# Attention chunks with float32 products with the values, two heads side by side, and 1/sum ahead of the transposition

## The chip, the core and the metric

The kernel runs on one core of a Trainium2 chip. The core has a matrix engine (TensorE, PE in the profile; its weight loads are listed as PEld), VectorE (DVE), ScalarE (ACT), GpSimd (POOL) and SyncE (SP), which here only issues transfers. TensorE writes to PSUM banks; the other three read and write the on-chip memory and, GpSimd excepted, PSUM. The metric is the device time of one execution in microseconds, as the median of repeated runs. Before the change it is 716.54 us (three runs, 716.34 to 716.68).

## What is computed

Attention with four sink keys and a window of 128 keys, in 4 batches and 8 heads of width 64 over 768 positions, followed by an expert layer with a squared ReLU. All data are float32.

```python
scores = scale * np.matmul(q, k.transpose(0, 1, 3, 2))
keep = is_sink | in_window
scores = np.where(keep, scores, -1000000000.0)
a = np.exp(scores - np.max(scores, axis=-1, keepdims=True))
a = a / (np.sum(a, axis=-1, keepdims=True) + 1e-09)
attn = np.matmul(a, v)            # (4, 8, 768, 64), then tokens x 512
h = x @ w_in                      # 3072 x 512 by 512 x 2048
r = np.maximum(h, 0.0)
g = s * (r * r) + b
out = g @ w_out
```

## The kernel before

**Tiling.** The 3072 tokens are worked in eight chunks of 384 (`CH`), half a batch each, in the order `ORDER`. A chunk of the first half of a batch is called half 0, one of the second half 1. Each chunk has an attention part, which leaves its result transposed in `k.x` (512 features x 384 tokens, as a high and a low part), and an expert part. The expert part of a chunk (`moe_steps`) consists of 16 blocks `l1(f)`, twelve products of 384 columns each (L610), and 16 blocks `l2(f)`, nine products of 512 columns each (L630), which alternate.

**Precision.** The fast products take float32r operands. A float32 number is therefore split into a rounded high part and the rest, and a product is made of high x high, high x low and low x high. Products of plain float32 operands also exist (L555 and L509 in the plain chunks); each is listed with two records in the profile.

**Order.** The instructions are recorded in program order on each engine, and a scheduler moves some of them. While the expert part of chunk c is recorded, the attention of chunk c+1 is recorded between its blocks in slots, some 33 for 30 blocks (the loop at L785). The first two chunks use the class `Plain`, which has float32 products throughout; chunks 2 to 7 use `attn_slots`. In a plain chunk, `values` multiplies the values two heads side by side: the head `hh` writes partitions 64*hh to 64*hh+63 of one bank (L555), and products of the same width spread 1/sum (L560).

**A slot in `attn_slots`.** The work on one head and 128 queries is a unit, 24 a chunk. In slot t, the kernel records what is due ahead (loads and `prep_head`), then `unit_c` for unit t-7 (`LC`), `unit_a` for unit t, `unit_b` for unit t-4 (`LB`), the ends of a group of heads, and the transposition `turn` for the next slot's `unit_b`.

- `unit_a` makes the scores (L308, L309), the masked minimum on VectorE (L313), the exponential with its row sum on ScalarE (L319), adds the two window squares into one on GpSimd (L322), since they don't overlap, and copies the eight sink columns to `psk` (L323).
- `turn` transposes the 128 x 128 square on TensorE (L329).
- `unit_b` splits the transposed square into its two triangles on VectorE (L342, into `two`), rounds the high part on ScalarE (L344) and makes the low part on GpSimd (L345), both into `hl`. After a pair's last unit it makes 1/sum (L354 to L358) and puts it into `psk`.
- `unit_c` multiplies by the values, in two visits a head: with the second unit (L382, four products in half 1, two in half 0) and with the third (L374 and two L382). The values stand side by side as high and low part in `vv` (128 wide), so that high and low come out in different partitions; L389, L390 and L392 add them.
- `sinks` adds the sink keys' part (L406, L407); `scaled` spreads 1/sum over the partitions by a product with `sel` (L413), multiplies (L414), and splits the result into `k.x` (L415, L416).

PSUM has eight banks: five rotate among the scores, `h`, `o`, `ts`, `os` and `zb` (pool `psA`, function `ps`), and three hold `po`. A bank is used again when its last reader is done.

Of the kernel before, what the change touches and what calls it, by code (L numbers as in the profile page):

```python
# [37 lines left out]
LB, LC, LD, LDL, L2 = 4, 7, ((3, 4), (6, 7)), ((2, 2), (3, 3)), 2  # L38
# [3 lines left out]
def tile_kernel(ctx, tc, qT, kT, k0, v, vsk, n_sink, window, w, s, b, out):  # L42
# [91 lines left out]
    def constants2():  # L134

        spread = wk.tile([P, 2, P], F32, tag="y", name="spread", bufs=3)
        nc.gpsimd.memset(spread, 0.0)
        for j in range(4):
            row = spread[96:P, j // 2].rearrange("p (a d) -> p a d", a=2)
            nc.gpsimd.affine_select(out=row, in_=row, pattern=[[1, 2], [0, D]], compare_op=ALU.not_equal, fill=1.0,  # L140
                                    base=2 * j, channel_multiplier=-1)
        nc.scalar.copy(sel, spread)
# [135 lines left out]
    def prep_head(k, h):  # L278
# [11 lines left out]
        hd.vv = wk.tile([P, 4, P], F32R, tag="vv", name="vv", bufs=VB)  # L290
        a, c = (0, D) if h % 2 == 0 else (D, 0)
        n = hd.nkb
        nc.scalar.copy(hd.vv[:, :n, a:a + D], hd.v[:, :n, :])
# [556 lines left out]
```

## Time and profile before

| | us |
|---|---|
| median of three runs | 716.54 |
| the profiled execution | 715.33 |
| its span | 713.6 |
| TensorE busy | 693.0 |
| VectorE busy | 500.6 |
| ScalarE busy | 469.4 |
| GpSimd busy | 385.3 |

The span runs from the first to the last instruction of the profiled execution; the rest of its time lies around it. The granted clock of TensorE was full (0.998) throughout. Up to about 130 us the first two chunks' attention and the preparation of the weights run; from there to about 635 us the expert part of chunks 1 to 6 runs with the attention of chunks 2 to 7 between its blocks; the last chunk's expert part stands alone. The time of a step on TensorE is read as the distance between the starts of two blocks in the timeline, since a matmul's listed duration overlaps that of the next. A line of a timeline stands for several records where it says x12.

### The profile page before, as it was taken

How to read it: one execution, taken by the hardware profiler on the slowest of the kernel's cores; microseconds unless marked ns; L12 is line 12 of the kernel's file. 1: busy time of each engine (PE TensorE's matmuls, PEld its weight loads, DVE VectorE, ACT ScalarE, POOL GpSimd, SP SyncE). 2: the span in 40 equal slices, each digit the busy share in tenths (PEclk: the TensorE clock that was granted, in tenths of full speed). 3: DMA queues.
4: the chain of work that ended last, by engine and by line, in shares of the span. 5: the costliest groups of instructions: out<-in, count | busy, mean ns of one | idle time of the engine just before them, and what ended most of it. 6: DMA issues, size and time to landing. Idle time of an engine off the chain costs nothing.

```text
span 713.6 us, 12060 instructions
## 1 busy us (share of the span) xinstructions
PE 693.0 (97%) x3908; PEld 613.8 (86%) x3908; DVE 500.6 (70%) x1186; ACT 469.4 (66%) x1153; POOL 385.3 (54%) x671
## 2 busy tenths in 40 slices
PE   8799999999999999999999999999999999999996
PEld 4477877899989998899999999899998999899895
DVE  6899979488865798657885788657786588743321
ACT  6999975578845786467764787556774677733222
POOL 2356635379843899336671788625773488700000
PEclk9999999999999999999999999999999999999999
DMA  7873140322112122021111121111221221000001
GB/s 283 355 269 130 34 155 27 108 66 57 57 56 75 42 81 55 17 82 58 50 57 65 51 72 51 35 64 53 57 63 37 80 66 42 1 30 15 1 1 49
DMA packets 27382, 52.63 MB, mean 74 GB/s; under 512 B 3504, under 2 KB 15536, under 8 KB 25392
## 3 DMA queue, kind: packets, MB, share of 16 engines
q1 hardware_dynamic: 27312, 51.79, 22.0%
q8 instruction: 33, 0.54, 0.3%
q14 instruction: 37, 0.30, 0.1%
HBM read 45.49 MB, written 6.29 MB: 73 GB/s over the span
## 4 chain that ended last, share of the span: by engine, by line
PE 76%; DVE 6%; ACT 3%; POOL 2%; issue 1%; DMA 1%; POOLq 0%; ACTq 0%; DVEq 0%
PE h L610 32%; PE po L630 32%; PE o L382 3%; PE sc L308 2%; PE sc L309 2%; PE sc L329 2%; DVE w L230 1%; DMA w<-in_w 1%; DVE w L220 1%; PE o L374 1%; DVE wt L219 1%; POOL hl L345 1%; POOL kl L289 1%; PE os L406 1%; PE ts L397 1%
## 5 line engine op out<-in xcount | busy, mean ns | idle before, releaser
L610 PE MATMUL h<-x,w 128*128 128x384 f32 x1536 | 297.6, 342 | 6.0 <-DVE w L230 2.6
L630 PE MATMUL po<-w,g 128*128 128x512 f32 x1152 | 295.9, 402 | 0.0
L610 PEld LDWEIGHTS h<-x,w 128*128 128x128 f32 x1536 | 264.8, 188 | 14.3 <-DVE w L230 3.3
L630 PEld LDWEIGHTS po<-w,g 128*128 128x128 f32 x1152 | 209.8, 189 | 43.7 <-issue 1.6
L616 DVE SCALAR_TENSOR_TENSOR r<-h,sb,r 128x384 f32<-128x384 f32 x112 | 68.9, 615 | 78.8 <-ACT r L613 77.9
L613 ACT ACTIVATE r<-h 128x384 f32<-128x384 f32 x128 | 62.9, 491 | 90.6 <-PE h L610 81.1
L619 DVE SCALAR_TENSOR_TENSOR g<-r,sb,g 128x384 fp32r<-128x384 f32 x112 | 91.5, 817 | 31.3 <-ACT g L618 29.7
L345 POOL TENSOR_TENSOR hl<-two,hl 128x256 fp32r<-128x256 f32 x128 | 102.3, 801 | 15.4 <-ACT hl L344 13.3
L322 POOL TENSOR_TENSOR sm<-sm 128x128 f32<-128x128 f32 x128 | 67.4, 527 | 61.2 <-ACT sm L319 59.0
L319 ACT ACTIVATE sm<-sm,negm 128x264 f32<-128x264 f32 (+1 forms) x144 | 72.1, 500 | 28.5 <-DVE negm L313 27.3
L618 ACT ACTIVATE g<-r,sb 128x384 fp32r<-128x384 f32 x112 | 69.1, 617 | 22.7 <-DVE r L616 21.9
L206 POOL TENSOR_TENSOR w<-w 128x256 int32<-128x256 int32 x60 | 48.6, 840 | 54.3 <-DVE zf L532 15.1
L289 POOL TENSOR_TENSOR kl<-kraw,kh 128x528 fp32r<-128x528 f32 (+1 forms) x48 | 60.8, 1266 | 20.7 <-ACT kh L287 20.4
L344 ACT CAST hl<-two 128x256 fp32r<-128x256 f32 x128 | 50.5, 394 | 26.0 <-DVE two L342 25.7
L342 DVE TENSOR_TENSOR two<-sc,split 128x256 f32<-128x256 f32 x128 | 53.1, 417 | 5.8 <-POOL hl L345 5.5
L323 POOL COPY psk<-sm 128x24 f32<-128x24 f32 x144 | 35.5, 247 | 17.1 <-ACT sm L319 17.0
L382 PE MATMUL o<-hl,vv 128*128 128x256 f32 (+1 forms) x256 | 44.3, 275 | 0.0
L382 PEld LDWEIGHTS o<-hl,vv 128*128 128x128 f32 x256 | 39.6, 188 | 3.2
L288 DVE TENSOR_TENSOR qs<-qraw,qs 64x384 fp32r<-64x384 f32 x48 | 39.7, 827 | 3.5 <-ACT qs L284 1.9
L313 DVE CUSTOM_DVE_ANT_0 sm<-sc,msk 128x264 f32<-128x264 f32 (+1 forms) x80 | 32.0, 400 | 14.0 <-PE sc L309 13.4
L308 PE MATMUL sc<-kh,qs 128*128 128x264 f32 (+1 forms) x144 | 41.6, 291 | 0.0
L313 DVE CUSTOM_DVE_ANT_0 sm<-sc,m_all 128x264 f32<-128x264 f32 x64 | 27.3, 426 | 20.1 <-PE sc L309 18.4
(139 smaller groups left out, 924.0 us busy)
## 6 DMA issues: line engine op xcount, KB each, us to landing
w<-in_w SPq DMA_DIRECT2D x15, 1024.0 KB, 10.5
kraw<-in_kT SPq DMA_DIRECT2D x32, 264.0 KB, 2.6
out<-ot SPq DMA_DIRECT2D x24, 256.0 KB, 2.0
qraw<-in_qT SPq DMA_DIRECT2D x24, 192.0 KB, 2.4
vraw<-in_v SPq DMA_DIRECT2D x16, 256.0 KB, 2.7
kraw<-in_kT SPq DMA_DIRECT2D x16, 200.0 KB, 2.4
vsraw<-in_vsk SPq DMA_DIRECT2D x24, 64.0 KB, 2.1
vraw<-in_v SPq DMA_DIRECT2D x8, 192.0 KB, 2.4
```

Of the source, the lines that this page charges most:

```text
L289: nc.gpsimd.tensor_tensor(out=hd.kl[:, :kw], in0=hd.k[:, :kw], in1=hd.kh[:, :kw].bitcast(F32), op=ALU.subtract)
L313: nc.vector.tensor_tensor_reduce(out=sm[:, :n], in0=sc[:, :n], in1=m, scale=-0.125, scalar=BIG, op0=ALU.add, op1=ALU.min, accum_out=negm[: ...
L319: nc.scalar.activation(sm[:, :n], sm[:, :n], AF.Exp, bias=negm[:, uu], scale=-1.0, accum_out=pp.zz[:, i, hh:hh + 1])
L322: nc.gpsimd.tensor_tensor(out=sm[:, c1:c1 + P], in0=sm[:, p1:p1 + P], in1=sm[:, c1:c1 + P], op=ALU.add)
L345: nc.gpsimd.tensor_tensor(out=lo, in0=both, in1=hi.bitcast(F32), op=ALU.subtract)
L382: nc.tensor.matmul(hd.o[:, q0:q0 + n * P], hd.vv[:, kb, :], hd.hl[:, t, c0 * P:(c0 + n) * P], start=(hd.n == 0), stop=(i == BLK - 1 and kb ...
L610: nc.tensor.matmul(h[:, :CH], weight[f][:, 0, wi, cc * P:(cc + 1) * P], x[xi][:, cc, :], start=(i == 0), stop=(i == 11))
L613: nc.scalar.activation(r, h[:, :CH], AF.Relu, scale=1.0 / WUP)
L616: nc.vector.scalar_tensor_tensor(out=hr, in0=h[:, :CH], scalar=sw_ap, in1=r, op0=ALU.mult, op1=ALU.mult)
L618: nc.scalar.activation(gg[:, 0, :], hr, AF.Identity, bias=b_ap, scale=1.0)
L619: nc.vector.scalar_tensor_tensor(out=gg[:, 1, :], in0=hr, scalar=b_ap, in1=gg[:, 0, :].bitcast(F32), op0=ALU.add, op1=ALU.subtract)
L630: nc.tensor.matmul(po[tb], gg[:, gi, tsl], weight[f][:, 1, wi, :], start=(f == 0 and i == 0), stop=(f == NF - 1 and i == 2))
```

## The change

It affects chunks 2 to 7.

- `unit_c` no longer works on rounded parts. It multiplies float32 squares by float32 values, once for both heads of a pair, when the second head's unit is due: each head writes its 64 partitions of one bank `o`, as in the plain chunks. The copies and additions of high and low parts (`vv`, `hl`, L389 to L392) go; `o` is copied once.
- A new step `norm`, in every second slot, makes 1/sum for two units on VectorE, multiplies their squares by it on ScalarE ahead of the transposition, and their sink columns on GpSimd, where these were copied before. `scaled`, `sel` and the places of 1/sum in `psk` go; `sinks` makes `k.x` itself.
- The values of a pair are loaded later, in a step of their own, six slots into the pair, with two buffers.
- `unit_b` and `unit_c` come one slot later (`LB` 5, `LC` 8), with five buffers `sm` instead of four. `hl` becomes `tt`, one for both heads.

```diff
-SMB, HLB = 4, 2
+SMB, HLB, VL = 5, 2, 6
-LB, LC, LD, LDL, L2 = 4, 7, ((3, 4), (6, 7)), ((2, 2), (3, 3)), 2
+LB, LC, LD, LDL, L2 = 5, 8, (3, 5), (2, 2), 2
...
+    def load_values(k, pr):
+
+        pp = k.pairs[pr]
+        pp.v = wk.tile([P, 4, 2, D], F32, name="v", tag="vv", bufs=2)
+        nc.sync.dma_start(pp.v[:, :pp.nkb], v[k.b, pr, :, pp.v0:pp.v0 + pp.nkb])
...
-        hd.vv = wk.tile([P, 4, P], F32R, tag="vv", name="vv", bufs=VB)
-        a, c = (0, D) if h % 2 == 0 else (D, 0)
-        n = hd.nkb
-        nc.scalar.copy(hd.vv[:, :n, a:a + D], hd.v[:, :n, :])
-        nc.gpsimd.tensor_tensor(out=hd.vv[:, :n, c:c + D], in0=hd.v[:, :n, :], in1=hd.vv[:, :n, a:a + D].bitcast(F32),
-                                op=ALU.subtract)
...
+    def norm(k, *two):
+
+        z = k.pairs[two[0][0] // 2].z
+        j0 = two[0][0] % 2 * BLK + two[0][1]
+        jj = slice(j0, j0 + 2)
+        nc.vector.tensor_scalar(out=z[:, 1, jj], in0=z[:, 0, jj], scalar1=1e-9, scalar2=None, op0=ALU.add)
+        nc.vector.reciprocal(out=z[:, 2, jj], in_=z[:, 1, jj])
+        for j, (h, i) in enumerate(two):
+            pp = k.pairs[h // 2]
+            sm, c0, _, s0 = k.cc[(h, i)]
+            rz = z[:, 2, j0 + j:j0 + j + 1]
+            nc.scalar.mul(sm[:, c0:c0 + P], sm[:, c0:c0 + P], rz)
+            nc.gpsimd.tensor_scalar(out=pp.psk[:, i, :12 * NS].rearrange("p (t x) -> p t x", t=3)[:, :, h % 4 * NS:(h % 4 + 1) * NS],
+                                    in0=sm[:, s0:s0 + NS].unsqueeze(1).to_broadcast([P, 3, NS]), scalar1=rz, scalar2=None, op0=ALU.mult)
...
         if p0 is not None:
-            both = wk.tile([P, 2 * P], F32, tag="two", name="two", bufs=2)
             nc.vector.tensor_tensor(out=both.rearrange("p (s c) -> p s c", s=2), in0=tp.unsqueeze(1).to_broadcast([P, 2, P]), in1=split,
                                     op=ALU.mult)
-            nc.scalar.copy(hi, both)
-            nc.gpsimd.tensor_tensor(out=lo, in0=both, in1=hi.bitcast(F32), op=ALU.subtract)
         else:
-            nc.scalar.copy(hi, tp)
-            nc.vector.tensor_tensor(out=lo, in0=tp, in1=hi.bitcast(F32), op=ALU.subtract)
...
+            nc.scalar.copy(both[:, P:], tp)
...
+        if h % 2 == 0 or i == 0:
+            return
         if i == 1:
...
+            pp.o = ps("o")
+        mm = [(cur - 1, 2 * i - 1, 2)]
         if i == 1 and k.half == 1:
             mm.append((0, 0, 1))
+        if i == BLK - 1:
+            mm.insert(0, (cur, 2 * i + 1, 1))
         for kb, c0, n in mm:
...
+            q0 = c0 // 2 * P
+            for hh in range(2):
+                nc.tensor.matmul(pp.o[hh * D:(hh + 1) * D, q0:q0 + n * P], pp.v[:, kb, hh], pp.t[:, hh, c0 * P:(c0 + n) * P],
+                                 start=(i == 1 and kb == cur - 1), stop=(i == BLK - 1 and kb == cur - 1))
...
-        zb = ps("zb")
-        nc.tensor.matmul(zb[:, :CH], sel[:, pr % 2], pp.xs, start=True, stop=True)
-        nc.vector.tensor_tensor(out=pp.x, in0=zb[:, :CH], in1=pp.x, op=ALU.mult)
...
+                if t % 2 == 0 and 0 < t <= n:
+                    norm(k, *units[t - 2:t])
```

The line numbers of the changed kernel differ: its score products are L298 and L299, `turn` is L331, the products with the values L363, `l1` L578 and `l2` L598. First TensorE in a half-1 chunk, where a head's values are multiplied before the change; `o` is the bank, `hl` the split squares, `vv` the values, `sc` the scores:

```order
L382 MATMUL o<-hl,vv 128x256 x2
L382 MATMUL o<-hl,vv 128x128 x2
L308 MATMUL sc<-kh,qs 128x264
L309 MATMUL sc<-kl,qs 128x264
L329 MATMUL sc<-identr,sm 128x128
L630 MATMUL po<-w_696,g 128x512 x9
L374 MATMUL o<-hl,vv 128x256
L382 MATMUL o<-hl,vv 128x256 x2
L308 MATMUL sc<-kh,qs 128x264
L309 MATMUL sc<-kl,qs 128x264
L329 MATMUL sc<-identr,sm 128x128
```

After it, where both heads of a pair are multiplied (`tt` holds their squares, `v` their values):

```order
L363 MATMUL o<-tt,v 64x256 x2
L363 MATMUL o<-tt,v 64x128 x2
L298 MATMUL sc<-kh,qs 128x264
L299 MATMUL sc<-kl,qs 128x264
L331 MATMUL sc<-identr,sm 128x128
L598 MATMUL po<-w_615,g 128x512 x9
L363 MATMUL o<-tt,v 64x128 x2
L363 MATMUL o<-tt,v 64x256 x2
L298 MATMUL sc<-kh,qs 128x264
L299 MATMUL sc<-kl,qs 128x264
L331 MATMUL sc<-identr,sm 128x128
```

The two visits of each head have become two visits a pair, each between full-width products of the expert part and of the scores; the products are 64 wide.

Now ScalarE in such a chunk before the change, with the exponential L319, the high parts L344, the Relu L613 and the bias copy L618 of `l1`:

```order
L319 ACTIVATE sm,zz<-sm,negm 128x264
L344 CAST hl<-two 128x256
L319 ACTIVATE sm,zz<-sm,negm 128x264
L344 CAST hl<-two 128x256
L613 ACTIVATE r<-h 128x384
L287 CAST kh<-kraw 128x528
L618 ACTIVATE g<-r,sb 128x384
L319 ACTIVATE sm,zz<-sm,negm 128x264
L344 CAST hl<-two 128x256
```

And after it, with the exponential L307, the Relu L581 and the bias copy L586 (`zz` holds the sums and 1/sum):

```order
L307 ACTIVATE sm,zz<-sm,negm 128x264
L324 ACTIVATE sm<-sm,zz 128x128 x2
L581 ACTIVATE r<-h 128x384
L280 CAST qs<-qraw 64x384
L307 ACTIVATE sm,zz<-sm,negm 128x264
L586 ACTIVATE g<-r,sb 128x384
L283 CAST kh<-kraw 128x528
L307 ACTIVATE sm,zz<-sm,negm 128x264
L324 ACTIVATE sm<-sm,zz 128x128 x2
L581 ACTIVATE r<-h 128x384
```

A high part per unit has gone; in every second slot two multiplications (L324) stand between an exponential and the Relu.

## Rows read from the trace of the kernel before

**Rows 1.** The page, busy us of each engine, share of the span and instructions.

```profile
PE 693.0 (97%) x3908; PEld 613.8 (86%) x3908; DVE 500.6 (70%) x1186; ACT 469.4 (66%) x1153; POOL 385.3 (54%) x671
```

**Rows 2.** Busy time by engine, stage with half-1 attention (stretch, us, busy us, records).

```profile
215.36:300.69 85.33, 84.84 (x479) 77.74 (x479) 62.73 (x148) 58.03 (x149) 58.27 (x104) 1.00 0.19 56
```

**Rows 3.** Chain that ended last, stage without attention (start us, us, what).

```profile
645.80 2.11 PE po L630 x9
647.91 2.12 PE h L610 x12
```

**Rows 4.** TensorE's timeline, half-1 attention, blocks alone (start us, us, engine line op).

```profile
234.13 2.36 PE L610 MATMUL h<-x,w 128*128 128x384 f32 x12
...
236.60 2.35 PE L630 MATMUL po<-w,g 128*128 128x512 f32 x9
...
239.52 2.37 PE L610 MATMUL h<-x,w 128*128 128x384 f32 x12
...
242.36 2.35 PE L630 MATMUL po<-w,g 128*128 128x512 f32 x9
```

**Rows 5.** TensorE's timeline, two visits of a half-0 chunk.

```profile
324.01 0.40 PE L382 MATMUL o<-hl,vv 128*128 128x256 f32 x2
324.25 0.28 PE L308 MATMUL sc<-kh,qs 128*128 128x264 f32 x1
...
326.71 0.28 PE L374 MATMUL o<-hl,vv 128*128 128x256 f32 x1
...
327.07 0.23 PE L308 MATMUL sc<-kh,qs 128*128 128x136 f32 x1
```

**Rows 6.** TensorE's timeline, a product with `sel`.

```profile
282.18 0.34 PE L413 MATMUL zb<-xsk,sel 128*128 128x384 f32 x1
282.35 0.27 PE L329 MATMUL sc<-identr,sm 128*128 128x128 f32 x1
```

**Rows 7.** TensorE's timeline, plain chunk, two visits of 64-wide products.

```profile
73.79 2.28 PE L630 MATMUL po<-w,g 128*128 128x512 f32 x9
76.00 1.52 PE L555 MATMUL o<-tf,vf 128*64 128x384 f32 x12
77.35 0.82 PE L560 MATMUL zb<-identr,zf 128*64 128x128 f32 x12
78.10 2.36 PE L610 MATMUL h<-x,w 128*128 128x384 f32 x12
80.30 0.49 PE L544 MATMUL tp<-identr,smf 128*128 128x128 f32 x3
...
108.66 2.25 PE L610 MATMUL h<-x,w 128*128 128x384 f32 x12
...
115.14 0.51 PE L610 MATMUL h<-x,w 128*128 128x384 f32 x2
```

**Rows 8.** Groups by line and shape, TensorE (busy us, mean ns | idle before).

```profile
L555 PE MATMUL o<-tf,vf 128*64 128x256 f32 x16 | 2.4, 379 | 0.0
...
L555 PE MATMUL o<-tf,vf 128*64 128x128 f32 x16 | 1.6, 273 | 0.0
```

**Rows 9.** Waits of TensorE, 131 to 640 us; then groups of weight loads.

```profile
PE h L610 <- DVE y L414: 1.9, 3, 1.1
...
L329 PEld LDWEIGHTS sc<-identr,sm 128*128 128x128 f32 x144 | 20.2, 140 | 1.7 <-DVE r L616 1.6
```

**Rows 10.** TensorE's timeline, plain chunk, one form of product twice.

```profile
80.83 0.92 PE L509 MATMUL sc<-kf,qf 64*128 64x384 f32 x4
...
99.10 1.31 PE L509 MATMUL sc<-kf,qf 64*128 64x384 f32 x4
```

**Rows 11.** Groups by line, page (VectorE, GpSimd); ScalarE by shape, 130 to 640 us.

```profile
L342 DVE TENSOR_TENSOR two<-sc,split 128x256 f32<-128x256 f32 x128 | 53.1, 417 | 5.8 <-POOL hl L345 5.5
...
L289 POOL TENSOR_TENSOR kl<-kraw,kh 128x528 fp32r<-128x528 f32 (+1 forms) x48 | 60.8, 1266 | 20.7 <-ACT kh L287 20.4
...
L275 ACT CAST vs<-vsraw 128x128 fp32r<-128x128 f32 x24 | 6.5, 293 | 0.0
```

More of the change, by code (lines that the diff above doesn't have):

```diff
@@ L30 @@
 LOADS = 8
-SMB, HLB = 4, 2
+SMB, HLB, VL = 5, 2, 6
 WARM0 = 14
 NARROW, NEARLY = 2, 8
-RB, VB = 1, 2
+RB = 1
 E0 = 16
@@ L134, in constants2 @@
     def constants2():
[L136 to L142, printed above, removed]
         nc.vector.tensor_tensor(out=tmp[:, :NS], in0=low[:, :NS], in1=snk[:, :NS], op=ALU.mult)
@@ L331, in unit_b @@
     def unit_b(k, h, i, tp):
-        sm, c0, p0, _ = k.cc.pop((h, i))
-        hd = k.heads[h]
-        if i == 0:
-            hd.hl = wk.tile([P, 2, 2 * CH], F32R, name="hl", tag="hl", bufs=HLB)
-        a, z = (P if p0 is None else 0), 2 * P
-        hi, lo = (hd.hl[:, t, i * z + a:(i + 1) * z] for t in range(2))
+        _, _, p0, _ = k.cc.pop((h, i))
+        pp = k.pairs[h // 2]
+        if h % 2 == 0 and i == 0:
+            pp.t = wk.tile([P, 2, 2 * CH], F32, name="tt", tag="hl", bufs=HLB)
@@ L360, in unit_c @@
     def unit_c(k, h, i):
-        hd = k.heads[h]
         pp = k.pairs[h // 2]
         cur = i if k.half == 0 else i + 1
+        if h % 2 == 0 or i == 0:
+            return
         if i == 1:
-            hd.o = ps("o")
-            hd.n = 0
-        mm = []
-        if i == BLK - 1:
-            c0 = (2 * i + 1) * P
-            nc.tensor.matmul(hd.o[:, i * P:], hd.vv[:, cur, :], hd.hl[:, :, c0:c0 + P], start=False, stop=False)
-        if i > 0:
-            mm.append((cur - 1, 2 * i - 1, 2))
+            pp.o = ps("o")
@@ L377, in unit_c @@
+        mm = [(cur - 1, 2 * i - 1, 2)]
         if i == 1 and k.half == 1:
             mm.append((0, 0, 1))
+        if i == BLK - 1:
+            mm.insert(0, (cur, 2 * i + 1, 1))
         for kb, c0, n in mm:
-            for t in range(2):
-                q0 = c0 // 2 * P
-                nc.tensor.matmul(hd.o[:, q0:q0 + n * P], hd.vv[:, kb, :], hd.hl[:, t, c0 * P:(c0 + n) * P],
-                                 start=(hd.n == 0), stop=(i == BLK - 1 and kb == cur - 1 and t == 1))
-                hd.n += 1
@@ L385, in unit_c @@
-        if i == BLK - 1:
-            a, c = (0, D) if h % 2 == 0 else (D, 0)
-            if h % 2 == 0:
-                pp.x = wk.tile([P, CH + P], F32, tag="y", name="y", bufs=3)
-            nc.scalar.copy(pp.x[a:a + D], hd.o[c:c + D])
-            nc.vector.tensor_tensor(out=pp.x[a:a + D], in0=hd.o[a:a + D], in1=pp.x[a:a + D], op=ALU.add)
-            if h % 2 == 1:
-                nc.gpsimd.tensor_tensor(out=pp.x[:, CH - P:CH], in0=pp.x[:, CH - P:CH], in1=pp.x[:, CH:], op=ALU.add)
-                pp.x = pp.x[:, :CH]
+            q0 = c0 // 2 * P
@@ L431, in attn_slots @@
             t = 4 * BLK * (pr // 2 + 1) - 1 + LC
-            for d, fn in zip((LD if pr < H // 2 - 2 else LDL)[pr % 2], (sinks, scaled)):
-                ends.setdefault(t + d, []).append((fn, pr))
+            ends.setdefault(t + (LD if pr < H // 2 - 2 else LDL)[pr % 2], []).append((sinks, pr))
         def slot(t):
@@ L454, in slot @@
             return f
-        parts = [slot(t) for t in range(n + LC + LDL[1][1])]
+        parts = [slot(t) for t in range(n + LC + LDL[1])]
         parts.pop(n + LB)
```

33 lines of the change are left out of this document (10 added, 23 removed).

## Prediction

> **What bounds the kernel now.** I read the busy table first, then busy time by stage, then TensorE's timeline. The table has TensorE busy for 97% of the span [rows 1]. The stage view says where that holds: in the stage from 215 to 301 us, in which the attention of a half-1 chunk runs between the steps of the expert layer, TensorE is busy 84.84 of 85.33 us while GpSimd, the engine that the change relieves most, works 58.27 [rows 2]. So between about 130 and 635 us a saving on another engine counts only where TensorE waits for it, and every nanosecond of TensorE counts whole. I therefore count TensorE from start to start: a matmul's own duration contains a pipeline that overlaps the next one.
>
> Without attention, nine products of `l2` take 2.11 us and twelve of `l1` 2.12 [rows 3]. With one unit (two score products and a transposition) a step takes 236.60 - 234.13 = 2.47 us [rows 4].
>
> **What the change removes on TensorE.** The values of a half-1 head come in two visits. In [rows 4] the first visit (four L382) lies behind the second block, whose step takes 239.52 - 236.60 = 2.92 us, 0.45 more than the plain step; the second visit (L374 and two L382) lies behind the third, whose step takes 242.36 - 239.52 = 2.84, 0.37 more. A head is 0.82, a pair 1.64 us. In a half-0 chunk the first visit has two products: 324.25 - 324.01 = 0.24; the second, 327.07 - 326.71 = 0.36 [rows 5]. A pair is 1.20. The product with `sel` that spreads 1/sum costs 282.35 - 282.18 = 0.17 a pair [rows 6]. Chunks 2 to 7 hold 16 half-1 and 8 half-0 pairs: 16 x 1.81 + 8 x 1.37 = 39.9 us go.
>
> **What it adds on TensorE.** Per pair there are again two visits, now with float32 products that write 64 partitions each, two heads side by side. The kernel before already has this form: L555 in the plain chunks, which L560 (also 64 wide) follows. The profile has two records for each such product (16 for eight in a chunk), and a record grows by 379 - 273 = 106 ns per 128 columns [rows 8]. A side-by-side product of 128 columns thus streams 0.21 us for both heads, one of 256 columns 0.42. A half-1 visit has 384 columns (0.64 us), a half-0 one 256 or 384. That is 40 visits x 0.64 + 8 x 0.42 = 29.0 us.
>
> The streaming alone would be 10.9 us less than what goes. But each visit changes the shape in which the array is used, and [rows 7] show what that costs. From 73.79 to 80.30 there are nine `l2`, twelve L555, twelve L560 and twelve `l1` records: 6.51 us. The two plain blocks account for 4.23, the streaming of L555 (768 columns) 1.27 and of L560 (384 columns) 0.64, so 0.37 is left over. It lies at four places: before L555 (2.21 instead of 2.11), in L555 (1.35 for 1.27), before the way back (L560 0.75 for 0.64) and in the first plain block after it (2.20 for 2.12). The second visit, 108.66 to 115.14, has 6.48 - 6.14 = 0.34. I take 0.35 for entering and leaving together. In the new program all 48 visits stand alone among full-width products (48 entries and 48 exits in its TensorE order): 48 x 0.35 = 16.8 us. Added: 29.0 + 16.8 = 45.8. **TensorE gets +5.9 us.**
>
> A rule of the Trainium skill speaks to this place. "TensorE: Matmul & The Clock Gate", section "Measured speedup vs the span model", prices packed products at one product's duration plus some 4 ns for each further tile, with no charge for coming and going; by that the 16.8 would be nearly nothing. "TensorEngine Tiling (Array Packing)", section "Key Properties", says that a change of tiling mode drains the engine; with it the rows agree (0.34 and 0.37 us a visit). The first rule is a rival below.
>
> **Waits that go.** In chunks 2 to 7 `l1` waits 1.9 us in three places for L414 on VectorE, which frees the PSUM bank of `zb`, and the weight loads of L329 wait 1.6 us for L616 [rows 9]. Both come from a VectorE that is late: L342 stood idle 5.8 us, 5.5 of it behind GpSimd's low parts at L345 [rows 11]. The change removes L345, L414 and the `zb` bank, and needs one bank `o` per pair instead of two. All of it could go (3.5), or none if VectorE finds something else to be late for; I take 2.5, since L414 and its bank vanish for certain while L616 stays.
>
> **What moves on the other engines.** Per unit, ScalarE loses the copy to `hl` and gains the multiplication of 128 x 128 squares by 1/sum; the nearest row is a 128 x 128 copy of 0.29 us [rows 11]. VectorE loses four small operations, two additions and a multiplication a pair, and gains six small ones. GpSimd loses L345, the low parts of the values and an addition; its sink copy becomes a multiplication of the same size. The values are loaded six slots into the pair, six before use, and SP's queue keeps its number of loads; the wait for making `vv` drops out of it. All this lies beside TensorE and is costed at nothing. The cover is the lead: a square is multiplied two or three slots (about 5 us) ahead of its transposition, and `tt` is written three slots ahead of its products. The chunk still ends in 33 slots, and behind the last sink product stand two `l2` blocks (4.2 us) before `l1` of the next chunk needs `x`; an addition, a copy and a subtraction per pair have to fit in, fewer than before. The new wait is ScalarE's: the multiplication waits for VectorE's reciprocal and for GpSimd's addition, and behind it in ScalarE's queue stand the Relu and the bias copy of `l1`, for which `l2` waits. Chunks 0 and 1 and the last stage keep their work; the mask `sel` was made within the first microseconds, on engines that then waited anyway: 0.
>
> **Sum.** +5.9 - 2.5 = +3.4 us. The profiled execution of before took 715.33 us (span 713.6 and 1.7 around it), 1.21 less than the median of the runs; so 718.7 for a profiled execution and 716.54 + 3.4 = 719.9 for the median.
>
> **Rivals.**
> 1. Crossings are cheaper than in the plain chunks. Place: the 48 visits. For it: the next weights can be fetched while something else runs, and a visit beside a transposition might hide part. Against it: both visits of [rows 7] show the full price after either kind of block, with weights that were long there. At no charge the change gives 716.54 + 29.0 - 39.9 - 2.5 = 703.1; at half, 711.5. The span rule of the Trainium skill named above stands behind the first of these figures. It is the price of a visit that decides the sign: below (39.9 + 2.5 - 29.0) / 48 = 0.28 us a visit the kernel isn't slower. Between 0.25 and 0.30 the time is 715.1 to 717.5, no change to be seen (a measurement of this kernel can tell 0.2%, 1.4 us, from none).
> 2. The two heads don't run side by side, so that the change doesn't do what it says. [rows 10] show L509, the sister form, once at 1.31 us for four records where 0.92 is usual: its second product had a wait of its own that was not yet met. In the new program only the two visits of a chunk's last pair, 12 in all, have such a wait. If it bites in all of them: 12 x 0.4 = 4.8, hence 724.7. If no visit ran side by side: 29.0 more, 749; L555 speaks against that.
> 3. ScalarE waits at the new multiplication behind GpSimd, whose key parts take 1.27 us each [rows 11], and TensorE waits for the bank that Relu should have freed. Two key parts per pair make 48 occasions; at 0.15 each that is +7, so 727. Against it: GpSimd loses more than it gains, and ScalarE, 58.03 us busy in 85.33 [rows 2], has a third of the stage free.
>
> **How the numbers follow.** The forecast, slower at 717.5 to 723, gets 0.66. Cheaper crossings get 0.22, of which 0.12 land within 0.2% and 0.10 faster; serialised visits 0.06; the new wait 0.06. With 0.04 of the forecast's own lower edge within 0.2%: faster 0.10, same 0.16, slower 0.74. The low end, 715.6, is a crossing of 0.28 with all 3.5 us of waits gone (716.54 + 29.0 + 13.4 - 39.9 - 3.5); below it lie the faster cases of rival 1. The high end, 724.7, is rival 2 in its 12 visits, which is also above the forecast with none of the waits gone (722.4); beyond it lies the new wait.
>
> **What would show it.** Right: a timeline of the new kernel in which a plain block before a visit takes 0.1 more, the visit some 0.7 to 0.8 with its way back, and the block or score product behind it another 0.1; half-0 stages longer by about 1.6 us (4 x 0.39), half-1 stages by 0.7 (4 x 0.17) less the waits that go there; no row "`l1` waits for" a sink product's bank. Wrong: visits of 0.64 us that leave their neighbours alone, visits of 1.1 us or more, or TensorE rows that wait for ScalarE's squares. What would make the sum wrong without touching its mechanism is the 2.5 us of waits, the one term that I chose by judgement.

## The result, and the profile after

The changed kernel takes 723.23 us (median of four runs, 721.57 to 724.38); the kernel before takes 716.44 beside it (716.26 to 716.68). The ratio is 1.0093, with a 95% interval of 1.0072 to 1.0113: slower, by some 6.8 us where 3.4 were forecast. That is inside the range of 715.6 to 724.7, just above the band of 717.5 to 723 that the prediction called its own forecast. The profiled execution took 721.57 us, its span is 719.4.

The page, first part: busy time of each engine, share of the span and instructions. It answers to [rows 1].

```profile
PE 698.4 (97%) x3932; PEld 590.5 (82%) x3932; DVE 447.4 (62%) x1146; ACT 441.0 (61%) x1096; POOL 269.5 (37%) x442
```

VectorE, ScalarE and GpSimd lost 53, 28 and 116 us of work. TensorE, which bounds the kernel, gained 5.4. The relief of three engines bought nothing.

Busy time by engine for two stages, from the first score product of a chunk to that of the next (stretch, us, then busy us and records of PE, PEld, DVE, ACT, POOL, granted clock, share of DMA, GB/s). First after, half-1 and half-0 attention; the half-1 line answers to [rows 2].

```profile
220.90:306.40 85.50, 85.26 (x483) 73.58 (x483) 54.86 (x143) 52.27 (x138) 38.16 (x63) 1.00 0.19 56
306.40:391.54 85.14, 84.01 (x467) 72.05 (x467) 49.44 (x135) 52.48 (x146) 31.37 (x55) 1.00 0.18 55
```

The half-0 stage of before, in the same view:

```profile
306.83:389.12 82.29, 82.29 (x464) 75.50 (x464) 59.59 (x147) 55.03 (x150) 47.17 (x87) 1.00 0.19 57
```

The half-1 stage shown is 0.2 us longer than before, the half-0 stage 2.9, of which TensorE idles 85.14 - 84.01 = 1.1; before, it idled in none of that stage.

TensorE's timeline of after, half-1 attention (start us, us, engine line op, [idle before <-releaser]). L598 is `l2`, L578 `l1`, L363 a visit of the new products, L298 and L299 the scores, L380 the sinks' product. It answers to [rows 4].

```profile
263.50 0.39 PE L298 MATMUL sc<-kh,qs 128*128 128x264 f32 x1
263.72 0.29 PE L299 MATMUL sc<-kl,qs 128*128 128x264 f32 x1
...
263.87 2.34 PE L598 MATMUL po<-w,g 128*128 128x512 f32 x9
266.15 0.87 PE L363 MATMUL o<-tt,v 128*64 128x128 f32 x8
266.95 0.55 PE L371 MATMUL ts<-identr,psk 128*128 128x128 f32 x3
...
270.06 2.35 PE L598 MATMUL po<-w,g 128*128 128x512 f32 x9
272.24 0.29 PE L298 MATMUL sc<-kh,qs 128*128 128x264 f32 x1
272.37 0.29 PE L299 MATMUL sc<-kl,qs 128*128 128x264 f32 x1
...
278.84 0.27 PE L331 MATMUL sc<-identr,sm 128*128 128x128 f32 x1
279.35 2.33 PE L578 MATMUL h<-x,w 128*128 128x384 f32 x12 [0.24 <-DVE tt L342]
```

The block ahead of a visit takes 266.15 - 263.87 = 2.28 us, an identical block ahead of scores 272.24 - 270.06 = 2.18: entering costs 0.10. The visit takes 0.80, 0.16 above the 0.64 of its columns in the prediction. A score product right behind a visit takes 263.72 - 263.50 = 0.22 where the plain one takes 0.13. That is 0.35 for entering, first product and leaving, as forecast, where scores follow. The last two rows are what the forecast had not: half a microsecond between a transposition and `l1`, behind VectorE's L342.

Waits of TensorE from 131 to 640 us (engine, tile and line <- what it waited for: us in total, times, longest). It answers to the first of [rows 9].

```profile
PE h L578 <- DVE tt L342: 3.9, 5, 1.4
```

The wait for L414 has gone with L414. A larger one came.

**Where the time went.** I added up, for the five stages from the first score product of chunk 2's attention to that of chunk 7's, the time from each TensorE product's start to the start of the next, by line. Before they last 556.73 - 135.30 = 421.43 us, after 562.44 - 134.69 = 427.75. The head is 0.6 shorter, the rest of the span 0.1 longer: 6.3 - 0.6 + 0.1 = 5.8 us of span, all from these stages. The other columns are experiments told below.

| us over five stages, against before | after | `keys_twice` | `no_extra_slot` | `one_visit` | `two_pairs` |
|---|---|---|---|---|---|
| old products with the values, and `sel` | -32.2 | -32.2 | -32.2 | -32.2 | -32.2 |
| new products with the values (L363 in after) | +30.3 | +30.3 | +30.3 | +27.3 | +25.8 |
| blocks of `l1` and `l2` | +3.9 | +4.2 | +3.3 | +2.1 | +2.0 |
| score products | +0.3 | +0.3 | +0.4 | -0.3 | -1.7 |
| transpositions of squares, with the waits behind them | +3.0 | -1.6 | -2.2 | -3.0 | -3.4 |
| products and transpositions of the sinks | +1.0 | +1.0 | +0.6 | +0.5 | +0.5 |
| sum | +6.3 | +2.0 | +0.2 | -5.6 | -8.9 |

### The profile page after: what moved, and what is told of

The parts are those of the page before. It is cut to its first block, busy times and chain, and to the rows that moved or that the text cites. A ratio compares the mean times of both kernels' runs of the same rounds, so it can differ in the third digit from the quotient of the medians.

```text
span 719.4 us, 11726 instructions
## 1 busy us (share of the span) xinstructions
PE 698.4 (97%) x3932; PEld 590.5 (82%) x3932; DVE 447.4 (62%) x1146; ACT 441.0 (61%) x1096; POOL 269.5 (37%) x442
## 4 chain that ended last, share of the span: by engine, by line
PE 75%; DVE 6%; ACT 5%; DMA 2%; POOL 2%; issue 1%; ACTq 0%; POOLq 0%
PE po L598 31%; PE h L578 31%; PE o L363 5%; PE sc L298 2%; PE sc L299 2%; PE sc L331 2%; DMA kraw<-in_kT 2%; POOL kl L285 1%; DVE w L221 1%; DVE g L587 1%; PE ts L371 1%; ACT g L586 1%; DMA w<-in_w 1%; DVE wt L210 1%; DVE w L211 1%
## 5 line engine op out<-in xcount | busy, mean ns | idle before, releaser
L578 PE MATMUL h<-x,w 128*128 128x384 f32 x1536 | 298.6, 343 | 8.1 <-DVE tt L342 3.9
L598 PE MATMUL po<-w,g 128*128 128x512 f32 x1152 | 295.5, 401 | 0.0
L578 PEld LDWEIGHTS h<-x,w 128*128 128x128 f32 x1536 | 265.5, 188 | 17.2 <-DVE w L221 3.3
L598 PEld LDWEIGHTS po<-w,g 128*128 128x128 f32 x1152 | 209.8, 189 | 45.0 <-issue 2.4
L311 POOL TENSOR_TENSOR sm<-sm 128x128 f32<-128x128 f32 x128 | 69.4, 542 | 153.7 <-ACT sm L307 86.7
L581 ACT ACTIVATE r<-h 128x384 f32<-128x384 f32 x128 | 62.3, 487 | 94.0 <-PE h L578 89.0
L587 DVE SCALAR_TENSOR_TENSOR g<-r,sb,g 128x384 fp32r<-128x384 f32 x112 | 79.9, 713 | 47.4 <-ACT g L586 46.1
L586 ACT ACTIVATE g<-r,sb 128x384 fp32r<-128x384 f32 x112 | 68.8, 615 | 36.2 <-DVE r L584 36.0
L307 ACT ACTIVATE sm<-sm,negm 128x264 f32<-128x264 f32 (+1 forms) x144 | 72.0, 500 | 29.3 <-DVE negm L303 28.7
L285 POOL TENSOR_TENSOR kl<-kraw,kh 128x528 fp32r<-128x528 f32 (+1 forms) x48 | 62.4, 1300 | 28.1 <-ACT kh L283 27.5
L324 ACT ACTIVATE sm<-sm,zz 128x128 f32<-128x128 f32 x144 | 49.9, 394 | 32.0 <-DVE zz L319 31.0
L325 POOL TENSOR_SCALAR psk<-sm,zz 128x24 f32<-128x24 f32 x144 | 56.8, 409 | 15.0 <-DVE zz L319 10.7
L342 DVE TENSOR_TENSOR tt<-sc,split 128x256 f32<-128x256 f32 x128 | 53.0, 417 | 13.9 <-PE sc L331 13.7
L383 POOL TENSOR_TENSOR x<-y,x 128x384 fp32r<-128x384 f32 x18 | 18.2, 1010 | 110.4 <-ACT x L382 110.4
L303 DVE CUSTOM_DVE_ANT_0 sm<-sc,msk 128x264 f32<-128x264 f32 (+1 forms) x80 | 32.2, 402 | 36.8 <-PE sc L331 19.2
L298 PE MATMUL sc<-kh,qs 128*128 128x264 f32 (+1 forms) x144 | 42.7, 299 | 0.0
L299 PE MATMUL sc<-kl,qs 128*128 128x264 f32 (+1 forms) x144 | 40.8, 285 | 0.0
L363 PE MATMUL o<-tt,v 128*64 128x256 f32 (+1 forms) x352 | 40.1, 344 | 0.0
```

What stands on the lines that cost most here:

```text
L285: nc.gpsimd.tensor_tensor(out=hd.kl[:, :kw], in0=hd.k[:, :kw], in1=hd.kh[:, :kw].bitcast(F32), op=ALU.subtract)
L298: nc.tensor.matmul(sc[:, :n], hd.qs[:, qs], hd.kh[:, c0:c0 + n], start=True, stop=False)
L303: nc.vector.tensor_tensor_reduce(out=sm[:, :n], in0=sc[:, :n], in1=m, scale=-0.125, scalar=BIG, op0=ALU.add, op1=ALU.min, accum_out=negm[: ...
L363: nc.tensor.matmul(pp.o[hh * D:(hh + 1) * D, q0:q0 + n * P], pp.v[:, kb, hh], pp.t[:, hh, c0 * P:(c0 + n) * P], start=(i == 1 and kb == cu ...
L578: nc.tensor.matmul(h[:, :CH], weight[f][:, 0, wi, cc * P:(cc + 1) * P], x[xi][:, cc, :], start=(i == 0), stop=(i == 11))
L581: nc.scalar.activation(r, h[:, :CH], AF.Relu, scale=1.0 / WUP)
```

## The experiments

Three things were to be told apart: what a visit costs (theory: 0.35 us each, which decides the sign; rival: much less), which part of the change costs what, and where the new wait comes from. The kernel before ran beside all of them at 715.6 to 716.3 us.

### What a visit costs

`crossings_in_before` is the kernel before with a stray pair of 64-wide products at 48 places; `full_width_in_before` has one 128-wide product there instead.

```diff
+        if i > 0 and h in (1, 3, 5, 6):
+            for a in range(2):
+                nc.tensor.matmul(k.bank[a * D:(a + 1) * D, 3 * P - 8:3 * P], ident[:, a * D:(a + 1) * D], ident[:, :8], start=True, stop=True)
```

```diff
+        if i > 0 and h in (1, 3, 5, 6):
+            nc.tensor.matmul(k.bank[:, 3 * P - 8:3 * P], ident, ident[:, :8], start=True, stop=True)
```

> The kernel before, with 48 extra visits of two 64-wide float32 products of 8 columns each into unused columns of a bank; results are unchanged. Theory A: each costs 0.34 for the change of shape and some 0.06 for four small records, 48 x 0.40 = 19 us, so 735.6. Theory B (hidden): the four records alone, some 3 us, so 719.

> Control for the run with extra visits: the kernel before, with 48 extra full-width float32 products of 8 columns, without a change of shape. By both theories two weight loads of 0.11 us each that nothing hides, 48 x 0.2 = 10 us at most, so 716.4 to 726. Theory A wants the run with 64-wide visits at least 7 us above this one, theory B wants it below (its weight loads are half as wide).

Measured: 732.51 us, 1.0226 of before (1.0200 to 1.0252), and 725.73, 1.0131 (1.0109 to 1.0154). Against 716.07 that is 16.4 us, 0.34 a place, and 9.7 us, 0.20 a place. The first lies 3 us below theory A's 735.6 and far from theory B's 719; the two are 6.8 us apart, where theory A wanted at least 7. TensorE's timeline with the 64-wide pair (L367) and, below, with the full-width product (L366), each time behind a block of `l1` and ahead of four products with the values:

```profile
247.76 1.40 PE L613 MATMUL h<-x,w 128*128 128x384 f32 x7
249.09 0.29 PE L367 MATMUL sc<-identr 128*64 128x8 f32 x4
249.31 0.68 PE L385 MATMUL o<-hl,vv 128*128 128x256 f32 x4
249.82 0.34 PE L308 MATMUL sc<-kh,qs 128*128 128x264 f32 x1
...
255.93 0.57 PE L385 MATMUL o<-hl,vv 128*128 128x256 f32 x4
256.34 0.34 PE L308 MATMUL sc<-kh,qs 128*128 128x264 f32 x1
```

```profile
247.64 2.37 PE L612 MATMUL h<-x,w 128*128 128x384 f32 x12
249.84 0.28 PE L366 MATMUL sc<-identr 128*128 128x8 f32 x2
249.98 0.65 PE L384 MATMUL o<-hl,vv 128*128 128x256 f32 x4
250.47 0.34 PE L308 MATMUL sc<-kh,qs 128*128 128x264 f32 x1
```

The stray pair takes 0.22 and makes the four products behind it 0.51 long instead of 0.41; the full-width one takes 0.14, makes them 0.49 long, and its block of 2.20 us is no longer than a plain one. So a good half of the price of these strays is that of a short float32 product that stands alone; the pair, which is also two products where the control has one, adds 0.14 us a place. The 0.34 is a total for this kind of visit and no pure price of the form. That the width has a part in it shows in TensorE's weight loads. The rows give the idle time ahead of them with nothing to wait for ("issue") from 131 to 640 us, in `crossings_in_before` and in after:

```profile
PEld sc L367 <- issue: 13.4, 48, 0.4
```

```profile
PEld o L363 <- issue: 10.1, 32, 0.4
```

Before each of the 48 stray pairs the weight load comes 0.28 us late on average, as if it could not be fetched ahead. In the list of `full_width_in_before`, whose products are float32 too, the stray product has no such row. The visits of the change need kernels that have fewer of them.

`one_visit` is the changed kernel with all products of a pair at its last unit, 24 visits instead of 48. `two_pairs` joins two pairs, 12 visits, with `unit_c` six slots behind the scores instead of eight.

```diff
-        if h % 2 == 0 or i == 0:
+        if h % 2 == 0 or i < BLK - 1:
             return
-        if i == 1:
-            pp.o = ps("o")
-        mm = [(cur - 1, 2 * i - 1, 2)]
+        pp.o = ps("o")
+        mm = [(cur - 2, 2 * i - 3, 2)]
...
+        mm += [(cur, 2 * i + 1, 1), (cur - 1, 2 * i - 1, 2)]
...
```

```diff
-LB, LC, LD, LDL, L2 = 5, 8, (3, 5), (2, 2), 2
+LB, LC, LD, LDL, L2 = 5, 6, (3, 5), (2, 2), 2
...
+        if h % 4 < 3 or i < BLK - 1:
+            return
+        for pp in (k.pairs[h // 2 - 1], k.pairs[h // 2]):
+            values_of(k, pp, cur, i)
...
```

> The changed kernel with all products of a pair made in one visit, at the second head's last unit: 24 visits of 64-wide products instead of 48, the same products. Theory A (each visit costs TensorE 0.34 us for the change of shape): 24 x 0.34 = 8.2 us less than the changed kernel's 723.2, so 715.0, a little faster than before. Theory B (the loss comes from the waits for VectorE, the change of shape is hidden): within 1.5 us of 723.2. In the trace A wants the plain blocks next to a visit unchanged (0.1 each longer) and half as many of them.

> The products of two pairs in one visit, 12 visits in all. To fit in memory the visit comes two slots earlier (LC 6), so the squares are ready one slot ahead instead of three. Theory A: 36 x 0.34 = 12.2 us less than 723.2, so 711.0; up to 3 us more if the shorter lead makes TensorE wait for VectorE. Theory B: 721.7 or more, since the lead is shorter and nothing else was lost to visits.

Measured: 709.80 us, 0.9909 of before (0.9888 to 0.9931), and 705.23, 0.9851 (0.9832 to 0.9871). The order is that of theory A, the gain is larger: 13.4 us below the changed kernel, then 4.6 more, where 8.2 and then 4.0 were expected. The trace splits it. Two stages of `two_pairs` in the view of [rows 2]:

```profile
218.57:301.54 82.97, 82.97 (x484) 74.09 (x483) 54.87 (x143) 53.05 (x138) 38.70 (x63) 1.00 0.20 58
301.54:383.37 81.83, 81.83 (x468) 72.94 (x468) 46.98 (x135) 52.80 (x146) 31.77 (x55) 1.00 0.20 57
```

TensorE idles in neither, and both are shorter than before. Over the five stages, `one_visit` spends 5.7 us less than `keys_twice`, another kernel without TensorE waits (below), on blocks, values and scores: 5.7 / 20 visits = 0.29 us a visit. `two_pairs` spends another 3.0 less on the same lines: 3.0 / 10 = 0.30. Against the changed kernel, the five stages of `one_visit` are 12.0 us shorter, and 6.0 of these are at the transpositions, where the waits were. Counted with everything that fell in the five stages, a visit less is worth more: 7.6 / 20 = 0.38 and 3.3 / 10 = 0.33 us; whether the 1.9 and 0.3 us at transpositions and sinks belong to the visits, no run separates. So a visit costs some 0.30 us on the lines beside it, and joining visits turns the change into a gain: `two_pairs` beats both kernels, the one before by 1.5%.

### The two parts alone

`values_only` is the kernel before with the new products with the values; 1/sum stays behind them, with `sel` and `scaled`, and there is no extra slot. `norm_only` is the kernel before with the new `norm` and the later slots, and the old rounded products.

```diff
+        if h % 2 == 0 or i == 0:
+            return
...
+            for hh in range(2):
+                nc.tensor.matmul(pp.o[hh * D:(hh + 1) * D, q0:q0 + n * P], pp.v[:, kb, hh], pp.t[:, hh, c0 * P:(c0 + n) * P],
+                                 start=(i == 1 and kb == cur - 1), stop=(i == BLK - 1 and kb == cur - 1))
...
```

```diff
+            nc.scalar.mul(sm[:, c0:c0 + P], sm[:, c0:c0 + P], rz)
...
-        zb = ps("zb")
-        nc.tensor.matmul(zb[:, :CH], sel[:, pr % 2], pp.xs, start=True, stop=True)
-        nc.vector.tensor_tensor(out=pp.x, in0=zb[:, :CH], in1=pp.x, op=ALU.mult)
...
+                if t % 2 == 0 and 0 < t <= n:
+                    norm(k, *units[t - 2:t])
```

> The kernel before with the first half of the change alone: float32 products with the values, two heads side by side, in 48 visits; 1/sum stays behind (product with sel, multiplication of the result), no extra slot. Theory A: TensorE loses the full-width visits (16 x 1.64 + 8 x 1.20 = 35.8 us) and gains 45.8, so +10.0; with the waits of before all gone 723.5 (716.5 + 10.0 - 3.0), with as many as before 726.5. Theory B (visits cost their streaming only, the loss comes from the multiplications by 1/sum): 716.5 + 29.0 - 35.8 = 709.7.

> The kernel before with the other half of the change alone: 1/sum multiplies squares and sink columns ahead of the transposition, one slot more; the products with the values stay full-width float32r in high and low parts. The product with sel and the multiplication behind it go. Theory A: 24 x 0.17 = 4.2 us of TensorE go and no visit changes the shape, so 712.2, between 709.7 (if the 2.5 us of waits also go) and 714.2 (if ScalarE's new multiplications bring 2 us of waits). If instead this half made the changed kernel slower, 718 or more.

Measured: `values_only` 722.15 us, 1.0082 (1.0060 to 1.0104), on the side of theory A, 1.4 us below the 723.5 that it gave with all waits gone; its trace has no TensorE wait from 131 to 640 us. `norm_only` 728.83, 1.0175 (1.0153 to 1.0198), where 712.2 was expected: a miss of 17 us. Its TensorE waits and two groups from 131 to 640 us (columns as before; groups: busy us, mean ns | idle before, releasers):

```profile
PE sc L333 <- DVE r L605: 8.6, 6, 1.6
PE o L368 <- POOL hl L349: 7.6, 6, 1.5
PE h L599 <- DVE r L605: 0.2, 1, 0.2
```

```profile
L349 POOL TENSOR_TENSOR hl<-two,hl 128x256 fp32r<-128x256 f32 x128 | 97.7, 763 | 17.3 <-ACT hl L348 16.7
L346 DVE TENSOR_TENSOR two<-sc,split 128x256 f32<-128x256 f32 x128 | 53.6, 419 | 12.7 <-POOL hl L349 9.4 <-PE sc L333 2.9
```

TensorE waits 16.4 us, nearly all of it once per chunk at two places: for the low parts that GpSimd makes (L349) and for VectorE's Relu step (L605). In this kernel ScalarE and GpSimd carry the multiplications and the high and low parts together. The 16.4 us account for most of the miss: without them it would be at 712.4, still 2.7 above the 709.7 that the expectation gave without waits. So the multiplication is not free by itself. In the changed kernel, where the new products take the high and low parts off ScalarE and GpSimd, TensorE has neither wait, and the two parts can't be added.

### Where the new wait comes from

`keys_twice` is the changed kernel with two buffers for the keys instead of one. The second plain chunk loads its keys under the same tag, so it gets two as well.

```diff
-        hd.k = wk.tile([P, 4 * P + 2 * NS], F32, tag="kraw", name="kraw", bufs=1)
+        hd.k = wk.tile([P, 4 * P + 2 * NS], F32, tag="kraw", name="kraw", bufs=2)
...
```

> The changed kernel with two buffers for a head's raw keys instead of one, so that their transfer starts before GpSimd has made the low parts of the keys ahead. Theory C (the new waits of TensorE for L342, 3.9 us, come from ScalarE's queue, where the rounding of the keys stands ahead of the bias copy and waits for that transfer): these waits fall below 2 us and the time to 719 to 721.5. Rival D (VectorE is late for reasons of its own order): the waits stay, 722.5 to 724.

The timeline of after around one of the five waits shows the suspect (columns as above; L283 copies the keys, L285 makes their low parts, L586 and L587 are the bias steps of `l1`, L342 empties the bank of the transposition).

```profile
357.17 0.64 ACT L283 CAST kh<-kraw 128x528 fp32r<-128x528 f32 x1
357.89 1.33 POOL L285 TENSOR_TENSOR kl<-kraw,kh 128x528 fp32r<-128x528 f32 x1 [0.63 <-ACT kh L283]
361.83 0.63 ACT L283 CAST kh<-kraw 128x528 fp32r<-128x528 f32 x1 [1.03 <-DMA kraw<-in_kT]
362.88 0.60 ACT L586 ACTIVATE g<-r,sb 128x384 fp32r<-128x384 f32 x1
363.51 0.80 DVE L587 SCALAR_TENSOR_TENSOR g<-r,sb,g 128x384 fp32r<-128x384 f32 x1 [1.11 <-ACT g L586]
364.24 0.41 DVE L342 TENSOR_TENSOR tt<-sc,split 128x256 f32<-128x256 f32 x1
364.70 1.48 PE L578 MATMUL h<-x,w 128*128 128x384 f32 x7 [1.13 <-DVE tt L342]
```

The next keys can only be fetched when GpSimd has finished with the single buffer, at 359.22. The transfer lands at 361.8, ScalarE's copy has waited 1.03 us for it, the bias copy behind it in ScalarE's queue is late, so VectorE's L587 is, so L342 behind that, and `l1` waits 1.13 us for the bank. The group of that copy from 180 to 560 us, before (L287), after, and in `keys_twice` (columns as above), one fence each:

```profile
L287 ACT CAST kh<-kraw 128x528 fp32r<-128x528 f32 (+1 forms) x34 | 19.6, 578 | 3.2 <-PE sc L308 3.0
```

```profile
L283 ACT CAST kh<-kraw 128x528 fp32r<-128x528 f32 (+1 forms) x34 | 19.5, 574 | 5.9 <-DMA kraw<-in_kT 4.7 <-PE sc L298 1.2
```

```profile
L283 ACT CAST kh<-kraw 128x528 fp32r<-128x528 f32 (+1 forms) x34 | 19.5, 575 | 1.2 <-PE sc L298 1.2
```

Measured: 719.29 us, 1.0047 (1.0032 to 1.0063), some 3.3 us below the changed kernel as ratios go. The copy no longer waits for a transfer, and TensorE's list of waits is empty. In the table, the line of the transpositions falls from +3.0 to -1.6. With a second buffer the wait is gone, so the single key buffer is what this order can't do with. It isn't enough by itself. In `one_visit`, which has one buffer, the same copy waits for the transfer as long:

```profile
L283 ACT CAST kh<-kraw 128x528 fp32r<-128x528 f32 (+1 forms) x35 | 20.1, 576 | 6.3 <-DMA kraw<-in_kT 5.0 <-PE sc L298 1.2
```

TensorE waits for nothing there: at the same place of the chunk a block of `l1` starts at 359.15 us, ahead of the late bias copy (359.58), so ScalarE's wait meets no block.

`no_extra_slot` is the changed kernel with the lead of before: `unit_b` four slots behind the scores instead of five, `unit_c` seven instead of eight, four buffers `sm`, the sinks asked for a slot earlier.

```diff
-SMB, HLB, VL = 5, 2, 6
+SMB, HLB, VL = 4, 2, 6
-LB, LC, LD, LDL, L2 = 5, 8, (3, 5), (2, 2), 2
+LB, LC, LD, LDL, L2 = 4, 7, (3, 5), (2, 2), 2
...
```

> The changed kernel without the one slot more (LB 4, LC 7, four buffers for the squares): a square of an even unit is multiplied one slot ahead of its transposition instead of two. If the lead of two slots is needed: TensorE waits at the transpositions for ScalarE, and the time is 725 or more. If one slot suffices: 721 to 724, the work on TensorE being the same.

Measured: 716.31 us, 1.0004 (0.9993 to 1.0016): no change against before, and 6 to 7 us under the changed kernel, where next to nothing or a loss was expected. Neither theory had it. ScalarE's copies of the keys in its timeline at the same place of the chunk:

```profile
356.23 0.62 ACT L283 CAST kh<-kraw 128x528 fp32r<-128x528 f32 x1
363.18 0.63 ACT L283 CAST kh<-kraw 128x528 fp32r<-128x528 f32 x1 [0.41 <-PE sc L298]
```

They are 363.18 - 356.23 = 6.95 us apart, in after 361.83 - 357.17 = 4.66, which is just the round of the buffer: 0.72 from the copy's start to that of the low parts, 1.33 for these, 2.61 to the end of the transfer. So here the keys come in time with one buffer. A chunk of after has 33 slots, as many as before, since the slot of `scaled` is saved; this one has 32. The number of slots isn't what brings the copies together, then: before, with 33, the same two stand 362.75 - 354.65 = 8.10 us apart. What places them so in after is not shown. Without the extra slot the waits go; 1.8 us per five stages below `keys_twice` remain, spread over blocks (0.95), transpositions (0.57) and sinks (0.45).

Is it the slot by itself? `values_and_slot` adds the extra slot to `values_only` (34 slots instead of 33), and `two_pairs_short` takes it from `two_pairs` (30 instead of 31).

```diff
-SMB, HLB = 4, 2
+SMB, HLB = 5, 2
-LB, LC, LD, LDL, L2 = 4, 7, ((3, 4), (6, 7)), ((2, 2), (3, 3)), 2
+LB, LC, LD, LDL, L2 = 5, 8, ((3, 4), (6, 7)), ((2, 2), (3, 3)), 2
...
```

```diff
-SMB, HLB, VL = 5, 2, 6
+SMB, HLB, VL = 4, 2, 6
-LB, LC, LD, LDL, L2 = 5, 6, (3, 5), (2, 2), 2
+LB, LC, LD, LDL, L2 = 4, 5, (3, 5), (2, 2), 2
...
```

> The kernel before with the new products with the values (as in the run with that part alone, 722.2 us and 1.0082 of before) and, added to it, the extra slot: the second part of a unit runs five slots behind its scores in place of four, the third eight in place of seven, and the sinks' values are asked for a slot later. Row factors stay with the squares of outputs, so that nothing else of the change is in it. Theory A: the slot itself costs, since taking it out of the changed kernel gave 7 us back (716.3 against 723.2); then this run is 2 to 7 us longer than 722.2, so 724 to 729, and either ScalarE waits again for the keys' transfer at its copy of the keys (over 3 us of it between 180 and 560 us) or the sum of the transposition's and the sinks' issue on TensorE is 1 us up. Theory B: the slot costs only together with the multiplications by 1/sum, which ScalarE and GpSimd do in it; then 722.2 plus or minus 1, and no wait of ScalarE for the keys' transfer over 1 us.

> The run with two pairs' products with the values made in one visit (705.2 us, 0.9851 of before) without the extra slot: the second part of a unit four slots behind its scores, the third five. Theory A (the slot costs by itself): 2 to 3 us less, 702 to 703.5; the part of the 7 us that was waits of TensorE is not to be had here, since that run had none. Theory B (the slot costs by those waits alone): 705.2 plus or minus 0.7.

Measured: 721.64 us, 1.0068 (1.0051 to 1.0085), and 711.14, 0.9920 (0.9903 to 0.9936). The first is the same as `values_only`, and its copy of the keys waits for no transfer, as theory B had it. The second is 5 us slower than with the slot, on a side that neither theory had. Its TensorE waits from 131 to 640 us:

```profile
PE sc L331 <- DVE r L585: 4.2, 5, 0.9
```

A timeline of one of them:

```profile
262.90 0.69 ACT L324 ACTIVATE sm<-sm,zz 128x128 f32<-128x128 f32 x2 [0.49 <-DVE zz L319]
263.50 0.47 ACT L582 ACTIVATE r<-h 128x384 f32<-128x384 f32 x1
264.00 0.62 DVE L585 SCALAR_TENSOR_TENSOR r<-h,sb,r 128x384 f32<-128x384 f32 x1 [1.20 <-ACT r L582]
264.68 0.33 PE L331 MATMUL sc<-identr,sm 128*128 128x128 f32 x1 [0.94 <-DVE r L585]
```

The two multiplications stand ahead of the Relu in ScalarE's queue, the Relu ahead of VectorE's L585, and the transposition waits for that one. So the slot has no price of its own: it costs nothing in `values_and_slot`, 6 to 7 us in the change, and it is worth 5 us in `two_pairs`. It shifts where the attention's steps fall between the blocks, and each kernel has another place where that hurts. Why the 1.8 us beyond the key wait go with the slot stays open; no run here separates them.

## Why the prediction was right, point by point

Right: the side, the range, and that the price of a visit sets TensorE's own work. Off: the size, 6.8 us where 3.4 were forecast, and the sign of the waits. For the five stages (40 of the 48 visits, 12 half-1 and 8 half-0 pairs) its steps read as follows.

- **What goes** on TensorE was 12 x 1.81 + 8 x 1.37 = 32.7 us by the prediction. Measured 32.2.
- **The streaming** was 32 x 0.64 + 8 x 0.42 = 23.8 us. The two heads do run side by side: a visit takes 0.80, so rival 2 is out, and with it its 12 visits.
- **The crossings** were 40 x 0.35 = 14.0. Measured, without the waits: L363 30.3, less 23.8 for its columns, plus 3.9 on the blocks, 0.9 on the first score products (the second ones lost 0.6 of wait) and 1.0 at the sinks: 12.3 us or 0.31 a visit. The form is right (0.10 ahead, 0.16 in the visit, 0.09 behind), but not every visit pays the last part in full. `one_visit` and `two_pairs` give 0.29 and 0.30. Rival 1, free crossings, is out: its 703.1 lies 20 us below the measured time; some 15 of these are the 48 visits at 0.31, the rest are waits. The span rule of the Trainium skill ("TensorE: Matmul & The Clock Gate", "Measured speedup vs the span model") stood behind that figure. At 0.3 the change loses, but only just: the prediction's break-even was 0.28.
- **The waits** were the term chosen by judgement, -2.5 us, and the step that failed. What it named did happen: the wait for L414 went, and in `keys_twice`, where nothing new stands in the way, the transpositions take 1.6 us less over the five stages than before and TensorE waits for nothing. But the changed kernel doesn't get it. The keys' single buffer is late, and the line of the transpositions is 3.0 up instead of down. In the prediction's terms, TensorE's own work over the five stages is +3.9 us (+5.1 forecast), and the waits are +2.4 (3.0 less the 0.6 at the scores) where the forecast had up to 2.5 less. One key buffer makes 4.6 us of the difference, against crossings some 2 us too dear over all 48 visits: the two errors partly cancel, and that the time lies inside the range is in part luck. Its upper end came from rival 2, which wasn't at work; with crossings as dear as forecast, the time would have been some 725.
- **"All this lies beside TensorE and is costed at nothing"** is where that wait should have been found. The prediction took ScalarE's and GpSimd's lower load as cover and looked at the multiplication's lead. It didn't ask how far apart two copies of keys come to stand in the new order, with one buffer whose round takes 4.66 us. No row of before shows ScalarE waiting there, and a small change of place made the wait; the sum of each engine's load didn't tell it.
- **Rival 3** named the right engine and the wrong release. The multiplication waits for VectorE's reciprocal (32.0 us idle before L324 on the page, 31.0 of it <- DVE L319), not for GpSimd, and nothing on TensorE comes of it in the changed kernel. In `norm_only` and `two_pairs_short`, where two multiplications stand ahead of the Relu in ScalarE's queue, TensorE does wait behind it, by way of VectorE's Relu step: 8.6 and 4.2 us.
- **The multiplication** was taken at 0.29 us from a copy of that size. It takes 0.39. The page after, groups of ScalarE's and GpSimd's new multiplications (busy us, mean ns | idle before, releaser):

```profile
L324 ACT ACTIVATE sm<-sm,zz 128x128 f32<-128x128 f32 x144 | 49.9, 394 | 32.0 <-DVE zz L319 31.0
...
L325 POOL TENSOR_SCALAR psk<-sm,zz 128x24 f32<-128x24 f32 x144 | 56.8, 409 | 15.0 <-DVE zz L319 10.7
```

  The Trainium skill had this price: "ScalarE: Activation LUTs", section "What ACT_TABLE_LOAD costs", gives 186 ns plus 0.833 ns an element of a partition for an ACTIVATE with constant scale and bias, and some 93 ns more for an operand of one value per partition. By it the copy is estimated at 293 ns and the multiplication at 386; the rows have 293 and 394. It moves nothing here, since ScalarE bounds no stage.
- **The stages**: half-0 ones were to grow by 1.6 us. The one shown grows by 2.9, of which 1.1 is idle. Half-1 ones were to grow by 0.7 less the waits; the one shown grows by 0.2.
- **The median** lies 1.7 us above the profiled execution, where the prediction added 1.2. The profiled run has a mean granted clock of 0.999, the other three 0.992 to 0.995 (below).

## What to carry to other kernels

When a kernel is bound by TensorE, count visits as well as columns: here a stay of half-width products among full-width ones cost some 0.30 us beyond its columns, so the same work took 716 to 723 us in 48 stays and 705 to 711 in 12, depending on the order of the rest. When steps are shifted, look at every buffer with a single copy and at its round (last reader, transfer, first user), since a load that comes in time gives no warning in the profile of before. Two parts of a change that share an engine are not worth the sum of what each is worth alone: one may make room for the other.

## What the runs showed of the hardware

The price of a lone product without columns: a single full-width product of eight columns cost 0.20 us at its place, though it streams almost nothing; the pair of 64-wide ones 0.34.

The granted clock falls to its lower level for a moment in some runs, at the start. In `keys_twice` (mean clock 0.995), three stretches of the start (us, busy us and records by engine, granted clock, share of DMA, GB/s):

```profile
20.00:25.00 5.00, 2.34 (x16) 1.03 (x12) 4.11 (x10) 5.00 (x17) 0.15 (x1) 0.91 1.03 431
25.00:30.00 5.00, 5.00 (x40) 3.45 (x38) 3.71 (x13) 4.25 (x10) 2.62 (x4) 0.74 1.00 401
30.00:35.00 5.00, 3.29 (x29) 1.82 (x25) 5.00 (x12) 5.00 (x13) 2.10 (x3) 1.00 0.77 278
```

TensorE was busy 2.34 of 5 us in the first stretch, with the DMA engines full, as they are in after; then the clock is at its level of 1.2 GHz for a part of the time, and at 2.4 GHz again by the third stretch. In the profiled run of after the first two of these stretches have 1.00:

```profile
20.00:25.00 5.00, 3.58 (x28) 2.16 (x28) 4.05 (x9) 5.00 (x13) 1.73 (x3) 1.00 1.01 426
25.00:30.00 5.00, 3.18 (x29) 2.03 (x28) 5.00 (x18) 5.00 (x16) 1.04 (x2) 1.00 1.00 402
```

The first score product of chunk 2's attention starts at 137.17 us in `keys_twice` and at 134.69 in after. The clock alone isn't shown to make that difference: in `two_pairs`, with a mean clock of 0.994, it starts at 135.61. The beginning differs from run to run, and so single runs are compared stage by stage here.
